# A depthwise-and-pointwise kernel: x's first chunk issued by ScalarE, and 28 satisfied waits on SyncE

## The chip, the cores and the metric

One core of a Trainium2 chip. The metric is the device time of one execution in microseconds (us), as the median of a kernel's runs. The span that the profile shows is about 1.7 us shorter than the device time of the same run (573.7 beside 575.44 us for the kernel before).

## The reference

x is (1, 384, 384, 384), dw is (1, 1, 384), pw is (384, 384), all bf16. With a window of one, the depthwise part is one factor for each channel:

```python
out = x * dw[0, 0]                       # each channel by its factor
return jnp.einsum('bhwc,cd->bhwd', out, pw)
```

The kernel folds dw into pw once, so that the rest is a single matrix product of 147456 rows of x with a 384 x 384 matrix.

## The kernel before

x is cut into 288 supertiles of 512 rows. VectorE transposes each (two halves), TensorE multiplies it with the folded weights (48 matmuls), ScalarE evicts it, SyncE loads and stores. Loads come in groups: the first is cut into chunks of 1, 1, 2, 2 and 4 supertiles so that work can start early, the next 26 are ten supertiles long. Three buffers of ten supertiles hold x, three hold the output.

```python
def load_x(t):
    g, i, off, first, L = chunks[t]
    ...                                   # dst: a slice of X buffer g % 3; src: rows of x
    if i == 0 and g >= NR:                # buffer free again?
        je = g_end[g - NR]
        nc.sync.wait_ge(s_t[je % 2][1], je // 2 + 1)
    nc.sync.dma_start(dst, src).then_inc(s_x[g % NR][i], 16)

def store(t):
    ...
    nc.sync.wait_ge(s_a[je % 2], je // 2 + 2)      # evicted?
    nc.sync.dma_start(dst, src).then_inc(s_o[g % NR], 16)

nc.scalar.dma_start(dw_row[:], ...).then_inc(s_dw, 16)
nc.sync.dma_start(pw_n[:], pw.rearrange("(k p) d -> p k d", p=P)).then_inc(s_pw, 16)
todo = []
for t, (g, i, off, first, L) in enumerate(chunks):
    todo.append((g_end[g - NR] if g >= NR else -1, load_x, t))
    todo.append((first + L + 1, store, t))
for _, f, t in sorted(todo, key=lambda a: a[0]):   # 7 loads first, then stores and loads in turn
    f(t)
...
# TensorE: idle matmuls, dw, idle matmuls, fold, main loop
nc.tensor.wait_ge(s_zero, 1)
idle_work(3)
...                                       # three tiny matmuls turn dw into a column
idle_work(3)
nc.tensor.wait_ge(s_pw, 16)
for k in range(3):                        # the fold: scaled selectors times pw
    nc.tensor.wait_ge(s_sw, k + 1)
    ...                                   # 18 matmuls in all; ScalarE and VectorE evict into w_r
with nc.tensor.Fori(0, NS // 2, 1) as it: # the main loop: 288 supertiles of 48 matmuls
    ...
# ScalarE: two warm copies, five evictions of the fold, then one eviction a supertile
# VectorE: selectors, one eviction of the fold, then two transposes a supertile
```

## Time and profile before

| | us |
|---|---|
| device time, median of 6 runs (lowest, highest) | 575.76 (575.40, 577.48) |
| span of the profiled run | 573.70 |
| pw landed | 4.05 |
| first matmul of the main loop | 7.18 |
| main loop, to the end of its last matmul | 561.81 |
| after it (eviction, last store, barrier) | 4.72 |

The last three rows, the start, the loop and the tail, 7.18 + 561.81 + 4.72, are the span. The prediction below shows the lines of the page, of the chain and of the timeline that carry this. The clock was granted in full in this profile at 6.82 us, before the loop began.

### The profile page before, as it was taken

Reading aid. Unit: us, or ns where it says so; the run is one execution under the profiler, and the core shown is the slowest. Engines: PE = TensorE matmul, PEld = TensorE weight load, DVE = VectorE, ACT = ScalarE, POOL = GpSimd, SP = SyncE. Lnnn points to the kernel's source line nnn. Section 1 sums busy time; section 2 is a strip of 40 time slices with the busy share of each in tenths; the row PEclk is TensorE's granted clock in tenths of the full one; section 3 lists DMA queues with packets and bytes.
Section 4 is the critical chain, followed back from the end, with each engine's and each line's share of the span. In section 5 each row is a group of like instructions: output and inputs, shape, how many; then the busy total and the mean of one; then the engine's idle time right before and its main releaser. Section 6 shows DMA issues by size and latency. Waiting matters only on the chain.

```text
span 573.7 us, 29706 instructions
## 1 busy us (share of the span) xinstructions
PE 567.3 (99%) x13869; PEld 414.9 (72%) x13869; DVE 509.3 (89%) x583; ACT 418.8 (73%) x296; POOL 0.9 (0%) x8
## 2 busy tenths in 40 slices
PE   8999999999999999999999999999999999999996
PEld 5777777777777777777777777777777777777774
DVE  6899999999999999999999999999999999999994
ACT  6777777777777777777777777777777777777775
POOL 0000000000000000000000000000000000000000
PEclk9999999999999999999999999999999999999999
DMA  8999999999999999999999999999999999994996
GB/s 324 432 409 417 430 397 430 444 424 422 399 408 416 384 397 436 398 383 395 432 398 384 395 429 390 393 401 429 402 385 419 401 390 397 425 394 149 402 408 251
DMA packets 25912, 226.88 MB, mean 395 GB/s; under 512 B 1197, under 2 KB 5678, under 8 KB 22062
## 3 DMA queue, kind: packets, MB, share of 16 engines
q1 hardware_dynamic: 25900, 226.79, 98.0%
q14 instruction: 9, 0.07, 0.0%
q8 instruction: 1, 0.02, 0.0%
q10 hardware_dynamic: 2, 0.00, 0.0%
HBM read 113.54 MB, written 113.25 MB: 395 GB/s over the span
## 4 chain that ended last, share of the span: by engine, by line
PE 98%; DMA 1%; ACT 0%; DVE 0%; issue 0%; SPq 0%
PE ps L166 97%; DMA pw_n<-in_pw_dram 1%; PE ps L216 1%; DMA out_dram<-O 0%; ACT O L307 0%; DVE O L304 0%; SPq L337 0%; SPq L100 0%
## 5 line engine op out<-in xcount | busy, mean ns | idle before, releaser
L166 PE MATMUL ps<-w_r,T 32*128 32x384 bf16 x13824 | 561.8, 321 | 0.1
L258 DVE STREAM_TRANSPOSE T<-X 128x384 uint32<-128x384 uint32 x576 | 506.2, 882 | 54.0 <-DMA X<-in_x_dram 2.4
L307 ACT CAST O<-ps 128x1536 bf16<-128x1536 f32 x288 | 413.5, 1436 | 147.9 <-PE ps L166 147.9
L166 PEld LDWEIGHTS ps<-w_r,T 32*128 32x128 bf16 x13824 | 412.9, 93 | 149.2 <-issue 0.7
L271 ACT CAST w_r<-ps 128x768 bf16<-128x768 f32 x5 | 3.7, 805 | 1.7 <-PE ps L216 1.6
L183 PE MATMUL ps<-zero 32*128 32x384 bf16 x24 | 2.6, 494 | 1.4 <-POOL zero L232 1.4
L304 DVE CAST O<-ps 128x768 bf16<-128x768 f32 x1 | 1.0, 958 | 3.0 <-DMA out_dram<-O 3.0
L216 PE MATMUL ps<-pw_n,sel_w 64*128 64x384 bf16 x18 | 3.0, 510 | 0.1
L183 PEld LDWEIGHTS ps<-zero 32*128 32x128 bf16 x24 | 0.7, 100 | 2.6 <-issue 2.6
L216 PEld LDWEIGHTS ps<-pw_n,sel_w 64*128 64x128 bf16 x18 | 1.2, 138 | 1.6 <-issue 1.2
L244 ACT ACT_TABLE_LOAD x1 | 1.3, 1283 | 1.5 <-SPq L100 1.5
L276 DVE TENSOR_REDUCE sel<-eye 128x64 f32<-128x128 bf16 x1 | 0.3, 290 | 1.8 <-POOL eye L234 1.8
L271 DVE CAST w_r<-ps 128x768 bf16<-128x768 f32 x1 | 1.0, 956 | 1.0 <-PE ps L216 1.0
L286 DVE TENSOR_SCALAR sel_w<-sel,dw_f 128x256 bf16<-128x256 f32 x3 | 0.9, 348 | 0.0
L283 DVE COPY dw_f<-ps 128x3 f32<-128x3 f32 x1 | 0.2, 161 | 0.8 <-PE ps L198 0.8
L198 PEld LDWEIGHTS ps<-ones,dw_row 1*128 1x128 bf16 x3 | 0.2, 98 | 0.2 <-issue 0.2
L244 ACT COPY warm<-warm 128x1 f32<-128x1 f32 x2 | 0.3, 188 | 0.0
L234 POOL TENSOR_SCALAR_AFFINE_SELECT eye<-ones 128x128 bf16<-128x128 bf16 x1 | 0.3, 292 | 0.1
L232 POOL MEMSET zero<- 128x192 uint32 x1 | 0.3, 258 | 0.0
L198 PE MATMUL ps<-ones,dw_row 1*128 1x1 bf16 x3 | 0.2, 159 | 0.0
L233 POOL MEMSET ones<- 128x128 bf16 x1 | 0.2, 204 | 0.0
L231 POOL MEMSET warm<- 128x3 f32 x1 | 0.1, 101 | 0.5 <-SPq L100 0.5
(4 smaller groups left out, 0.4 us busy)
## 6 DMA issues: line engine op xcount, KB each, us to landing
X<-in_x_dram SPq DMA_DIRECT2D x26, 3840.0 KB, 21.5
out_dram<-O SPq DMA_DIRECT2D x26, 3840.0 KB, 27.5
X<-in_x_dram SPq DMA_DIRECT2D x2, 1536.0 KB, 17.4
out_dram<-O SPq DMA_DIRECT2D x2, 1536.0 KB, 13.7
X<-in_x_dram SPq DMA_DIRECT2D x3, 768.0 KB, 8.8
out_dram<-O SPq DMA_DIRECT2D x3, 768.0 KB, 8.9
X<-in_x_dram SPq DMA_DIRECT2D x1, 2304.0 KB, 18.9
out_dram<-O SPq DMA_DIRECT2D x1, 2304.0 KB, 12.1
```

The source lines that it names most:

```text
L166: mm = nc.tensor.matmul(PS[s][:, q, :D], lhsT=Ts[s][32 * q : 32 * q + 32, b, par::2], rhs=w_r[32 * q : 32 * q + 32, b, par, :], start=(b, ...
L183: nc.tensor.matmul(PS[0][:, i, :D], lhsT=zero[32 * i : 32 * i + 32, 0:P], rhs=zero[32 * i : 32 * i + 32, :], start=True, stop=True, tile_p ...
L198: mm = nc.tensor.matmul(PS[1][:, 0, D + k : D + k + 1], lhsT=dw_row[:, P * k : P * k + P], rhs=ones[0:1, 0:1], start=True, stop=True,)
L216: mm = nc.tensor.matmul(PS[(k + 1) % 2][:, 2 * r + v, :D], lhsT=sel_w[64 * v : 64 * v + 64, k, r, :, :].rearrange("p q w -> p (q w)"), rhs ...
L232: nc.gpsimd.memset(zero[:].bitcast(U32), 0).then_inc(s_zero)
L234: nc.gpsimd.affine_select(out=eye[:], in_=ones[:], pattern=[[-1, P]], compare_op=mybir.AluOpType.is_equal, fill=0.0, base=0, channel_multi ...
L244: c = nc.scalar.copy(warm[:, s + 1 : s + 2], warm[:, 0:1])
L258: ins = nc.vector.transpose(out=Tw[:, 3 * h : 3 * h + 3], in_=Xw[:, :, j, 96 * h : 96 * h + 96].rearrange("p k (b w) -> p b k w", w=32),)
L271: o = nc.vector.tensor_copy(out, in_) if e == 0 else nc.scalar.copy(out, in_)
L286: nc.vector.tensor_scalar_mul(sel_w[:, k], sel[:].unsqueeze(2).to_broadcast([P, 2, 4, 32]), dw_f[:, k : k + 1]).then_inc(s_sw)
L304: e = nc.vector.tensor_copy(Ov[:, nq:4, j, :], PS[s][:, nq:4, :D])
L307: a = nc.scalar.copy(Ov[:, 0:nq, j, :], PS[s][:, 0:nq, :D])
```

## The change

Its intent is a faster start: ScalarE's queue is free when SyncE has pw and seven loads to issue, so the first chunk of x goes there, and SyncE gets to the second chunk half a microsecond sooner. The 28 waits, all satisfied by then, only lengthen SyncE's program ahead of its first store.

```diff
-        def load_x(t):
+        def load_x(t, eng=nc.sync):
...
-            nc.sync.dma_start(dst, src).then_inc(s_x[g % NR][i], 16)
+            eng.dma_start(dst, src).then_inc(s_x[g % NR][i], 16)
...
         nc.scalar.dma_start(dw_row[:], dw.rearrange("a e c -> a (e c)")).then_inc(s_dw, 16)
+        load_x(0, nc.scalar)
         nc.sync.dma_start(pw_n[:], pw.rearrange("(k p) d -> p k d", p=P)).then_inc(s_pw, 16)
...
-            todo.append((g_end[g - NR] if g >= NR else -1, load_x, t))
+            if t > 0:
+                todo.append((g_end[g - NR] if g >= NR else -1, load_x, t))
...
         for _, f, t in sorted(todo, key=lambda a: a[0]):
+            if f is store and t == 0:
+
+                for _ in range(28):
+                    nc.sync.wait_ge(s_pw, 16)
             f(t)
```

## The prediction

> **What bounds the kernel now.** I read four views of the profile of before, in this order: the page, to see which engine is full; the chain of work that ended last, to see which piece at the start and at the end counts; the busy time in four stretches, to see if the middle has any gap; and the timeline and the waits of the first microseconds, because everything in this change happens there.
>
> The page: TensorE is busy nearly all the time, and the chain that ended last is nearly all one line.
>
> ```profile
> PE 567.3 (99%) x13869; PEld 414.9 (72%) x13869; DVE 509.3 (89%) x583; ACT 418.8 (73%) x296; POOL 0.9 (0%) x8
> ...
> PE ps L166 97%; DMA pw_n<-in_pw_dram 1%; PE ps L216 1%; DMA out_dram<-O 0%; ACT O L307 0%; DVE O L304 0%; SPq L337 0%; SPq L100 0%
> ...
> L166 PE MATMUL ps<-w_r,T 32*128 32x384 bf16 x13824 | 561.8, 321 | 0.1
> L258 DVE STREAM_TRANSPOSE T<-X 128x384 uint32<-128x384 uint32 x576 | 506.2, 882 | 54.0 <-DMA X<-in_x_dram 2.4
> ```
>
> The last column is to be seen: TensorE idles 0.1 us before 13824 matmuls, so no wait inside the main loop costs anything. VectorE idles 54.0 us and is not the bound, although its transposes wait 2.4 us for loads.
>
> The chain in order of time (start, length, piece):
>
> ```profile
> 0.89 0.12 issue
> 1.01 3.03 DMA pw_n<-in_pw_dram
> 4.05 0.05 issue
> 4.09 2.96 PE ps L216 x18
> 7.05 0.12 issue
> 7.18 557.91 PE ps L166 x13728
> 565.08 0.02 issue
> 565.11 1.45 ACT O L307
> 566.55 0.02 issue
> 566.57 2.46 DMA out_dram<-O
> ```
>
> The kernel has three parts. Until 7.18 us it waits for the small matrix pw (issued at 1.01, landed at 4.05) and folds dw into it on TensorE. From 7.18 on it is matmuls alone: 13728 of them are 286 supertiles of 48, and 557.91 / 286 = 1.951 us each. All 288 take 561.8 us and end at 569.0. The rest, 573.7 - 569.0 = 4.7 us, is the last eviction, the last store and the closing barrier. The span is therefore 7.18 + 561.8 + 4.7 = 573.7 us.
>
> The same in stretches (columns: length, then busy time of each engine, then granted clock, DMA share, GB/s):
>
> ```profile
> 4.05:7.18 3.13, 2.96 (x19) 1.25 (x20) 2.23 (x3) 2.45 (x4) 0.00 (x0) 1.00 0.85 264
> 7.18:569.00 561.82, 561.78 (x13824) 412.87 (x13824) 504.80 (x575) 413.96 (x289) 0.00 (x0) 1.00 0.99 400
> ```
>
> TensorE is busy 561.78 of 561.82 us. The middle can get slower, but it can't get faster by moving a load. The DMA engines are full too (0.99), yet their work is ahead of TensorE's by whole buffers.
>
> **What the Trainium skill says.** "DMA: Bandwidth & Descriptors", section "Issuing engines are not separate DMA queues", says that transfers from the scalar and the sync queue run on the same 16 DMA engines and interleave, so that issuing from two engines saves issue time only. The trace before agrees on the size of that saving: consecutive issues on SyncE begin about 0.5 us apart (seven of them in 3.49 us). Section "Queues, rings and completion order" of the same page says that each DMA engine takes turns between the queues that have work, packet by packet. The trace before can't show this, since everything but dw goes through one queue. The prediction's sign rests on it. "TensorE: Matmul & The Clock Gate", section "Part 1: The HAM clock gate", says that TensorE's array runs at half clock until it has been busy for a window of about 3.4 us, and that the window runs free of the kernel's start. The trace agrees: taken one by one, the pairs of folding matmuls at 4.1 to 6.6 us begin 313 ns apart for 384 columns (1.2 columns a ns), and the groups of four in the main loop 162.5 ns apart (2.4 a ns).
>
> **The change, part by part.**
>
> 1. *x's first chunk leaves SyncE's queue.* SyncE's timeline is
>
> ```profile
> 1.01 0.45 SPq L132 DMA_DIRECT2D pw_n<-in_pw_dram  x1
> 1.52 3.49 SPq L113 DMA_DIRECT2D X<-in_x_dram  x7
> 10.82 2.35 SPq L128 DMA_DIRECT2D out_dram<-O  x2
> ```
>
> pw's issue stays at 1.01. The six other loads are issued some 0.5 us earlier. That buys no bytes: behind the issues the DMA engines are already full (0.85 of them busy from 4.05 to 7.18).
>
> 2. *ScalarE issues it after dw.* dw's issue takes 0.97 to 1.46, so x's first chunk is issued at about 1.5, where SyncE issued it at 1.52. ScalarE's own work moves back by one issue, 0.49 us: its table load from 1.49 to about 2.0, its two warm copies to an end at 3.6. Its first needed work, the eviction of the folded weights, starts at 4.63. So 1 us of slack remains and this costs nothing.
>
> 3. *x's first chunk now competes with pw.* This is the part on the path. Taking the DMA packets one by one, pw is 384 packets of 768 B that start from 2.12 on and end by 3.69 us. The chunk is 128 packets of 3072 B at 121 ns, which is 128 x 121 / 16 = 0.97 us of each DMA engine. Before, its first packet starts at 3.01, on an engine that has finished its part of pw. After, if it takes from issue to first packet what pw took (2.12 - 1.01 = 1.1 us), it starts at 1.5 + 1.1 = 2.6 us. By then 91 of pw's 384 packets had started; the other 293 would share with it. At worst all 0.97 us falls ahead of pw's last packets. But between 2.12 and 3.0 us the 229 packets of pw, of 47 ns mean, fill 10.8 of 16 x 0.88 = 14.1 us, so about a quarter of the time is free and takes up part of it. I choose 0.6 us later for pw, out of 0.2 to 1.0. Everything up to the main loop follows pw (0.05 + 2.96 + 0.12 = 3.13 us after it), so the loop starts at about 7.8 and the end moves by the same 0.6 us. Nothing gives it back, since the loop has no gap.
>
> 4. *28 satisfied waits on SyncE.* pw has landed by 4.05 before and by about 4.7 after, and SyncE gets there at about 4.5. Two plain waits at the end of the kernel begin 64 ns apart on SyncE; 28 x 64 = 1.8 us at most, an estimate (fewer if two fold into one instruction). They end near 6.5 us. The first store waits for the first eviction until 10.82, so 4 us of slack is left. Cost: nothing.
>
> Sum: 575.77 + 0.6 = 576.4 us.
>
> **The rivals.**
>
> *Earlier data helps.* The chunk's transposes start at 5.83, but it landed at 5.00: VectorE was busy until then with a folded weight (0.96 us from 4.96). The second chunk is what VectorE waits for:
>
> ```profile
> 8.00 1.57 DVE L258 STREAM_TRANSPOSE T<-X 128x384 uint32<-128x384 uint32 x2 [0.62 <-DMA X<-in_x_dram]
> ```
>
> Its half tile is ready at about 8.8, and the second supertile starts at 7.18 + 1.95 = 9.13, so there's no stall to remove. If pw somehow landed earlier with less queued behind it on its ring, the gain would be 0.1 to 0.3 us: 575.5.
>
> *A load becomes late.* The tightest one is the first long group: it lands at 25.16, its transposed half is ready at about 26.1, and supertile 10 starts at 7.18 + 10 x 1.95 = 26.68. Slack 0.6 us. The bytes ahead of it are the same as before, and a later start of the loop adds slack. I give this little weight; it would cost some tenths of a us.
>
> *The clock gate.* The idle matmuls end at 4.02, just as pw lands at 4.05. If pw is 0.6 us late, TensorE has a hole of that length in the window that should release the clock. If the release then misses its turn, up to 3.4 us of main loop run at half clock, which costs up to 1.7 us: 578.1. The three runs of before spread from 575.57 to 577.48, 1.9 us, which has the size of such a missed window, though no trace here shows that it is one. I give it one chance in six.
>
> *The waits push something else.* They lengthen SyncE's program and can move its instruction fetches. SyncE idles between transfers nearly everywhere, and nothing here reaches 1 us.
>
> **Range and chances.** The low end is no delay of pw plus run-to-run spread (575.3). The high end is 1.0 us of delay with a missed clock window for most of its 1.7 us (578.2). A change of 2% would be 11.5 us; no part of the change touches the 561.8 us of matmuls, so both outer chances are tiny.
>
> **What would show it.** After: the chain's piece for pw is longer than 3.03 us by the same amount by which the main loop starts after 7.18; 48 matmuls still take 1.95 us; the tail after the last matmul is still 4.7 us; SyncE's first store is still issued some 3.6 us after the loop's start. Step 3 is wrong if pw lands by 4.1 us. Step 4 is wrong if the first store comes later than 1.5 us after the first eviction's start. The whole is wrong if TensorE shows waits inside the loop.

## More of the kernel before

All runs that have a state were in the fast one. The five kernels that ran once (e4, e8, e9, e10, e12) have none; I read their profiles, and no verdict rests on their times.

## The result, and the profile after

The kernel after takes 575.87 us (median of 6 runs, 575.26 to 576.42), the kernel before 575.76 us (6 runs). The ratio is 0.9998 with a 95% interval of 0.9985 to 1.0012: no difference is to be seen. A ratio here is the mean time of one kernel's fast runs over the mean of the other's of the same rounds, so it is not quite the ratio of the medians.

The chain of the kernel after, in order of time (start, length, piece), to be held against the chain of before in the prediction:

```profile
...
2.84 1.18 PE ps L189 x12
4.01 3.00 PE ps L222 x18
7.02 0.02 issue
7.04 558.29 PE ps L172 x13728
565.33 0.02 issue
565.35 1.45 ACT O L313
566.80 0.02 issue
566.82 2.45 DMA out_dram<-O
```

The piece "DMA pw_n" is gone from the chain. pw landed at 3.91 us, 0.1 us before the last idle matmuls ended (4.01), so the chain now goes through these; the fold's first weight load still waits for pw and follows its landing by 0.04 us:

```profile
3.95 0.13 PEld L222 LDWEIGHTS ps<-pw_n,sel_w 64*128 64x128 bf16 x4 [0.34 <-DMA pw_n<-in_pw_dram]
```

The loop starts at 7.04, 0.14 us earlier than before, yet the same 13728 matmuls take 558.29 us in place of 557.91.

The stretches of before again, of the kernel after:

```profile
4.05:7.18 3.13, 3.11 (x22) 1.25 (x26) 2.36 (x4) 2.58 (x4) 0.00 (x0) 1.00 1.03 413
7.18:569.00 561.82, 561.82 (x13824) 384.16 (x13816) 503.00 (x575) 414.11 (x289) 0.00 (x0) 1.00 0.99 399
```

TensorE is as full as it was; the loop isn't slower because of a wait. In the first stretch the DMA engines moved 413 GB/s where they had moved 264. So loads did come earlier, which VectorE's timeline shows too:

```profile
4.82 0.96 DVE L277 CAST w_r<-ps 128x768 bf16<-128x768 f32 x1 [0.86 <-PE ps L222]
5.69 6.74 DVE L264 STREAM_TRANSPOSE T<-X 128x384 uint32<-128x384 uint32 x8
```

Eight transposes run without a wait. Before, two ran, then VectorE waited 0.62 us for the second chunk. That chunk landed at 7.97 us before and at 5.86 after; the first one landed later than before (5.58 in place of 5.00). And SyncE:

```profile
1.01 0.45 SPq L133 DMA_DIRECT2D pw_n<-in_pw_dram  x1
1.52 2.89 SPq L113 DMA_DIRECT2D X<-in_x_dram  x6
11.13 2.28 SPq L128 DMA_DIRECT2D out_dram<-O  x2
```

Taken one by one, the waits are 13 instructions of two waits each, 63 ns apart, from 4.47 to 5.25 us; the last two waits went onto the store's own instructions. The first store is issued 0.09 us after the end of the first eviction, where it had been 0.03.

Where the 0.24 us between the two profiles is: the loop's start gave 0.14 us; its first three groups of four matmuls took 272, 320 and 280 ns in place of 162, which cost 0.38 us; the tail is the same (4.71 and 4.72). The clock record explains the slow groups: full clock was granted at 7.87 us, after the loop's start, where before it was 6.82.

### The profile page after: what moved, and what is told of

Read it like the earlier page. It is cut to its first block, busy times and chain, and to the rows that moved or that the text cites. A ratio compares the mean times of both kernels' runs of the same rounds, so it can differ in the third digit from the quotient of the medians.

```text
span 573.9 us, 29720 instructions
## 1 busy us (share of the span) xinstructions
PE 567.8 (99%) x13869; PEld 386.3 (67%) x13869; DVE 507.6 (88%) x583; ACT 419.1 (73%) x296; POOL 0.9 (0%) x8
## 4 chain that ended last, share of the span: by engine, by line
PE 98%; DMA 0%; ACT 0%; DVE 0%; issue 0%; POOL 0%; POOLq 0%; SPq 0%
PE ps L172 97%; PE ps L222 1%; PE ps L189 0%; DMA out_dram<-O 0%; ACT O L313 0%; DVE O L310 0%; POOL zero L238 0%; POOL warm L237 0%; PE ps L204 0%; POOLq L343 0%; SPq L100 0%
## 5 line engine op out<-in xcount | busy, mean ns | idle before, releaser
L172 PEld LDWEIGHTS ps<-w_r,T 32*128 32x128 bf16 x13824 | 384.3, 93 | 178.2 <-issue 0.7
```

Source lines behind the costliest of these rows:

```text
L172: mm = nc.tensor.matmul(PS[s][:, q, :D], lhsT=Ts[s][32 * q : 32 * q + 32, b, par::2], rhs=w_r[32 * q : 32 * q + 32, b, par, :], start=(b, ...
```

## The experiments

Twelve experiments, in three batches and a single one; two are repeats of the two kernels. The record names another chip for each batch (1, 12, 5, and 7 for e12), and each ratio compares runs of one batch. First the table of all profiles, since the argument needs them side by side. "Clock" is when the record shows full clock granted (for e4 and e9, the second time: it had come at 4.90 and 5.83 and was withdrawn in the long wait for data). "Loop" is from its first matmul to the end of its last. All in us; GB/s is what the DMA engines moved from 5 to 8 us.

| kernel | pw landed | clock | loop starts | loop | tail | span | GB/s |
|---|---|---|---|---|---|---|---|
| before | 4.05 | 6.82 | 7.18 | 561.81 | 4.72 | 573.70 | 287 |
| before again (e8) | 4.11 | 7.52 | 7.24 | 561.92 | 7.42 | 576.58 | 338 |
| after | 3.91 | 7.87 | 7.04 | 562.19 | 4.71 | 573.94 | 419 |
| after again (e10) | 3.91 | 4.92 | 7.00 | 561.81 | 4.71 | 573.52 | 428 |
| move only (e1) | 4.04 | 7.62 | 7.17 | 562.00 | 4.82 | 574.00 | 430 |
| waits only (e2) | 3.95 | 4.98 | 6.89 | 561.80 | 5.90 | 574.59 | 270 |
| x before pw (e3) | 5.07 | 7.86 | 8.20 | 561.81 | 5.32 | 575.33 | 287 |
| no idle work (e5) | 3.94 | 9.62 | 7.22 | 562.97 | 4.71 | 574.89 | 281 |
| 400 waits (e6) | 4.10 | 6.32 | 7.23 | 561.81 | 4.72 | 573.76 | 420 |
| pw split (e7) | 4.15, last part | 6.48 | 6.67 | 561.81 | 4.71 | 573.18 | 390 |
| pw split again (e11) | 5.08, last part | 10.89 | 7.38 | 563.51 | 4.71 | 575.60 | 399 |
| long load on ScalarE (e4) | 3.98 | 18.55 | 15.43 | 563.32 | 4.92 | 583.67 | 371 |
| the same, later in program (e9) | 3.94 | 19.49 | 15.63 | 563.68 | 4.83 | 584.14 | 383 |
| small packets first (e12) | 6.82 | 11.27 | 9.95 | 562.43 | 6.14 | 578.53 | 352 |

To be read in it: in every row the span is loop start + loop + tail. The loop is 561.8 us plus, where the clock came after the loop's start, half of the time between, less some 0.04 us: after, (7.87 - 7.04) / 2 = 0.42 against 0.38; no idle work, (9.62 - 7.22) / 2 = 1.20 against 1.16; pw split again, (10.89 - 7.38) / 2 = 1.76 against 1.70.

### e1: the move alone

```diff
-            if f is store and t == 0:
-
-                for _ in range(28):
-                    nc.sync.wait_ge(s_pw, 16)
```

(against the kernel after)

> The move of x's first chunk alone, without the 28 waits. My theory: both parts of the change cost and gain nothing, and the 0.2 us between the two profiles is the phase of TensorE's clock (3 slow groups of four matmuls in the profile after, none before). Then the ratio to before is 1.000 within its interval, pw lands between 3.9 and 4.1 us, x's first packets on ScalarE's queue start only when each DMA engine has ended pw (3.2 us or later), and the loop's length is 561.8 us plus half of whatever part of it ran at half clock. Rival, cancelling parts: the move alone costs or gains some tenths (574.5 or 576.5 us) and the waits give it back. One thing open: the 8 KB instruction fetch seen at 569.07 us before and at 496.8 after is SyncE's if it moves one SyncE instruction later here, to about 570.0, beside the last store; if that stalls the store the tail after the last matmul grows from 4.71 to about 5.0 us.

Measured: 575.49 us (5 runs) beside 575.58 (9 runs of before); ratio 0.9993, interval 0.9979 to 1.0006. pw landed at 4.04, the chunk's first packet on ScalarE's queue started at 3.01, 58 ns after the first of the packets that tell of pw's completion (I had expected 3.2 or later), and two slow groups at the loop's start cost 0.19 us. The instruction fetch was at 570.82, where the profile of before had it at 569.07, and the tail was 4.82, not 5.0. The fetch's place says nothing of the move, since the unchanged kernel has it at 570.83 in e8. The move costs and gains nothing that timing shows.

### e2: the waits alone

```diff
         for _, f, t in sorted(todo, key=lambda a: a[0]):
+            if f is store and t == 0:
+
+                for _ in range(28):
+                    nc.sync.wait_ge(s_pw, 16)
             f(t)
```

(against the kernel before)

> The 28 waits alone, x's first chunk back on SyncE. My theory: ratio to before 1.000 within its interval; 13 or 14 wait instructions some 61 ns apart end near 5.9 us, the first store is issued within 0.15 us of the first eviction's end, and an instruction fetch appears near 480 to 500 us in place of the one at 569 us, with the tail unchanged at 4.7 us. Rival, cancelling parts: this alone is 0.5 us or more away from before, in the opposite direction of the move alone.

Measured: 575.27 us (5 runs) beside 575.58; ratio 0.9990, interval 0.9976 to 1.0003. Again there are 13 wait instructions, ending at 6.04 us, and the first store was issued at 10.60, 0.1 us after the end of the first eviction. SyncE's 8 KB fetch is at 495.88 us, so the waits move it away from the tail, as in the kernel after (496.79). That buys nothing: profiles with the fetch at 569.07, 567.40, 570.20 and 496.79 all have a tail of 4.71 or 4.72 us. This profile's tail was 5.90 because the last store landed late, which other profiles show without the waits (5.32 in e3). Two parts that cancel each other would have opposite signs. The intervals of e1 and e2 end at 0.35 and 0.2 us above before, so such parts could be a few tenths of a microsecond at most, and the profiles show none.

### e3: a control, x's first chunk ahead of pw

```diff
+        load_x(0)
         nc.sync.dma_start(pw_n[:], pw.rearrange("(k p) d -> p k d", p=P)).then_inc(s_pw, 16)
```

(against the kernel before; the chunk is left out of the list)

> A control that delays pw on purpose: x's first chunk is issued before pw on SyncE, so pw is behind its 0.97 us of packets and 0.5 us later in issue. My theory: pw lands at about 5.0 us, the loop starts 3.0 to 3.1 us after that (about 8.1), nothing gives it back, and the time is about 1.0 us above before (576.7), up to 1.7 us more where the clock is released late. Rival, pw is not what the start waits for: the loop starts by 7.4 us and the time stays within 0.3 us of before.

Measured: 576.83 us (5 runs, 576.62 to 577.22) beside 575.58; ratio 1.0017, interval 1.0003 to 1.0031. The chain:

```profile
1.47 3.61 DMA pw_n<-in_pw_dram
5.07 0.05 issue
5.12 2.96 PE ps L218 x18
8.08 0.12 issue
8.20 557.91 PE ps L168 x13728
```

pw is back in the chain. It landed 1.02 us later than in the profile of before, the loop started 1.02 us later, and the medians are 1.25 us apart. So a delay of pw does go through to the end. The timing of the kernel after alone would not have excluded the predicted 0.6 us (its interval goes up to 0.7 us above before); that of e1 does (up to 0.35), and pw's landing shows directly that there was no delay. It is the only timed kernel whose interval excludes 1.

### e4 and e9: a long load on ScalarE's queue

e4 puts the first ten-supertile load (3840 KB) in the place of the first chunk; e9 puts it after ScalarE's warm copies in the program.

```diff
-        load_x(0, nc.scalar)
+        load_x(5, nc.scalar)
...
-            if t > 0:
+            if t != 5:
```

(e4, against e1)

> The load of the first long group (3840 KB, ten supertiles) is issued by ScalarE after dw, the first chunk again by SyncE after pw, no waits: two queues with much work at once. Theory of issue order (whichever queue issued first is served first): the long load is issued at about 1.5 us, a hair before x's first chunk, so that chunk lands after some 9.8 us of the long load's packets, at about 14 us, and the kernel ends some 8 to 9 us later than before (584). Theory of taking turns packet by packet (what I predicted with): x's first chunk lands at about 6 us, the second at about 8, all of SyncE's early loads run at half rate until the long one is done at about 23 us, TensorE stalls only later, before supertile 6, by some 4 to 6 us (580).

Measured: one run, 585.39 us, span 583.67. VectorE and TensorE wait at the start:

```profile
PE ps L168 <- DVE T L260: 9.2, 1, 9.2
DVE T L260 <- DMA X<-in_x_dram: 8.6, 1, 8.6
```

The long load landed at 14.27 us, the first chunk at 14.45. That is the number of the "issue order" theory. Counting packet starts in each microsecond of the trace shows that it is wrong:

```
us         long load (30720 B)   first chunk (3072 B)
4 to 5             15                    14
5 to 6              7                    10
6 to 7             11                     9
7 to 8             15                    13
8 to 9             16                    16
9 to 10            15                    15
```

The two queues take turns, about one packet each. But a packet of the long load takes 1.14 us and one of the chunk 0.12, so the chunk, with as many packets (128), ends only when the long load does. My expectation for "taking turns" had silently assumed packets of equal size.

```diff
             c.then_inc(s_a[s])
+        load_x(5, nc.scalar)
```

(e9, against the kernel before with the load taken out of SyncE's list)

> The 3840 KB load again on ScalarE's queue, but issued after ScalarE's two warm copies, at about 3.1 us, between SyncE's issues of its fourth early load (2.98) and its fifth (3.45). Theory of issue order, now the leading one: the first chunk lands near 5, the second near 7.5, the third near 9.5, the fourth (two supertiles) near 11.5 us, all as before; the long load lands near 21, and only SyncE's fifth load is behind it, near 25 us, so TensorE stalls some 6 us at supertile 6. Rival, ScalarE's queue goes first whenever it has work: the long load lands near 14.5 us and the second, third and fourth chunks all land after 14 us. Rival, taking turns packet by packet: the second to fourth chunks land at about twice their time (10, 14, 18 us) and the long load near 22.

Measured: one run, 585.86 us, span 584.14. The experiment failed as designed: ScalarE's queue issued the load at 1.60 us, not 3.1, since the issue doesn't wait for the table load and the copies ahead of it (they ran until 3.1). So it repeats e4, with the load issued 0.08 us after the chunk and not just before it, and the outcome is the same: landings at 14.46 and 14.65. That the order of two issues so near each other doesn't matter fits taking turns.

### e5: no idle matmuls

```diff
-        nc.tensor.wait_ge(s_zero, 1)
-        idle_work(3)
...
-        idle_work(3)
```

(against the kernel before)

> The kernel before without its two blocks of idle matmuls, to size the clock. So far six profiles show the clock released at 4.9 to 7.9 us, 3.4 to 6.4 us after TensorE's first matmul at 1.43, and what ran after the loop's start at half clock cost half its length. Theory (a free-running window that must be filled by work): with no work before the fold at about 4.05 us, the release falls between 7.4 and 10.9 us; the loop starts at about 7.2 and loses half of what lies between, 0.1 to 1.8 us, 1.0 on average; median about 576.6 us and a wider spread. Rival (the release doesn't follow TensorE's own work): release stays between 4.9 and 7.9 us and the time within 0.2 us of before.

Measured: 576.01 us (6 runs, 575.32 to 576.91) beside 575.52 (11 runs); ratio 0.9998, interval 0.9979 to 1.0018, so timing alone decides nothing. The profile does: clock at 9.62, eight slow groups, the loop 1.16 us longer, inside the 0.1 to 1.8 expected. In this profile the first chunk of x landed late (6.22 us) and set the loop's start; that is a hazard of the original order too.

### e6: 400 waits

```diff
-                for _ in range(28):
+                for _ in range(400):
```

(against the kernel after)

> The changed kernel with 400 satisfied waits in place of 28: 200 wait instructions x 0.061 us = 12.2 us, so SyncE reaches its first store at about 16.7 us in place of 11.1. Theory (the waits are hidden, and even a late first store is): ratio to before 1.000 within its interval, loop still without gaps, tail 4.7 to 5.9 us as in the runs so far. Rival (SyncE's early order matters): the later stores and the fourth long load slip by 5 us, ScalarE or VectorE waits for a buffer, and the time rises by 1 us or more. It is also a third profile with x's first chunk on ScalarE's queue: if the higher DMA rate seen with it between 5 and 8 us (419 and 430 GB/s, against 287, 270 and 287 with all loads on SyncE) belongs to the move, it is above 400 here.

Measured: 575.42 us (4 runs) beside 575.52; ratio 0.9999, interval 0.9972 to 1.0026. The first store was issued at 17.48 us, 6.4 us later than in the kernel after, and the loop is gapless (561.81). The delay is gone by the third long load (the first that reuses a buffer), issued at 32.69 (32.48 before, 32.61 after): the issue of the third store ends only at 30 to 31 us in every case, after 14.6 us before and 11.5 here. What holds it isn't shown. Fourteen times the waits still cost nothing.

### e7 and e11: pw in three parts

```diff
-        nc.sync.dma_start(pw_n[:], pw.rearrange("(k p) d -> p k d", p=P)).then_inc(s_pw, 16)
+        for k, eng in enumerate((nc.sync, nc.scalar, nc.sync)):
+            eng.dma_start(pw_n[:, k, :], pw[P * k : P * k + P, :]).then_inc(s_pw[k], 16)
...
-        idle_work(3)
-        nc.tensor.wait_ge(s_pw, 16)
+        idle_work(1)
...
+            nc.tensor.wait_ge(s_pw[k], 16)
             nc.tensor.wait_ge(s_sw, k + 1)
```

(against the kernel before; s_pw becomes three semaphores)

This is the version that e3 points to: if pw's landing moves the end, an earlier pw should help.

> The kernel before with pw in three transfers of 128 rows, each with its own semaphore, the middle one on ScalarE's queue, and the second idle block cut from 3 rounds to 1. If the start hangs on pw's landing alone, the fold of the first third can begin at about 3.5 us, when its scaled selector is ready (3.43), the loop starts about 0.5 us earlier (6.6 us) and the time falls by 0.5 us to about 575.1, ratio 0.999, which 5 rounds may or may not show. Against it: the third transfer may land later than 4.05 us and the clock's phase moves the loop by up to 0.5 us either way.

> The kernel with pw in three transfers once more, with 5 more rounds. In its first profile the loop started at 6.67 us, 0.51 earlier than before, yet its timed median was 575.94 us. If the gain is there but small beside the spread of tail and clock, the profile again shows a loop start of 6.6 to 6.8 us and the ratio is between 0.998 and 1.000. If the first profile was luck, the loop starts at 7.0 or later.

Measured: e7 575.94 us (6 runs, 574.90 to 576.50), ratio 0.9999, interval 0.9979 to 1.0018; e11 575.69 (6 runs, 574.89 to 577.32) beside 575.55 (11 runs), ratio 0.9998, interval 0.9986 to 1.0011. In e7's profiled run the loop started at 6.67, as expected, and that run took 574.90 us. In e11's it didn't:

```profile
1.52 3.37 DMA pw_n<-in_pw_dram
4.88 0.05 issue
4.93 2.42 PE ps L217 x14
7.35 0.03 issue
7.38 559.61 PE ps L167 x13256
```

One third landed at 4.88 and another at 5.08, the fold's third pair of matmuls began 1.08 us after its second (0.3 us elsewhere), and the clock came only at 10.89 us: 1.70 us of the loop lost, and a run of 577.32. The gain of 0.5 us is there in one profiled run and lost in the other. No version that beats the two kernels came out.

### e8 and e10: the two kernels once more

No edit.

> The kernel before once more, unchanged, for a second profile. Expected: clock released anywhere between 4.8 and 8.2 us, loop 561.8 us plus half of what runs at half clock, tail 4.7 to 5.9 us, and the DMA rate between 5 and 8 us below 300 GB/s if the low rate belongs to the one queue and not to one unlucky run.

Measured: one run of 578.29 us, span 576.58, slower than any of the timed runs of before. Its loop took 561.92 us, so neither clock nor loads made it slow. The wait for the last stores did, which SyncE shows as

```profile
SPq L141 <- DMA out_dram<-O: 4.7, 1, 4.7
```

where the profile of before had 2.0 us. The DMA rate between 5 and 8 us was 338 GB/s, above the 300 that I had set, but well under those of the move.

> The changed kernel once more, unchanged: a fourth profile with x's first chunk on ScalarE's queue. Expected: pw lands at 3.9 to 4.1 us; DMA rate between 5 and 8 us above 400 GB/s; VectorE waits for no load; the time is loop start plus 561.8 us plus half of what runs at half clock plus a tail of 4.7 to 7.4 us, where the tail and the clock vary from run to run as they do with the kernel before.

Measured: one run of 575.24 us, span 573.52. 428 GB/s. Two things differ from what I expected. VectorE did wait for loads, 0.26 us for the first chunk and, in the loop, 0.28 us for the first long load at 23.99 us; TensorE didn't wait for it. And full clock came early, at 4.92, the fold was done by 6.17, and then the first chunk's landing set the loop's start.

```profile
1.52 4.50 DMA X<-in_x_dram
6.02 0.02 issue
6.04 0.87 DVE T L264
6.91 0.09 issue
7.00 557.91 PE ps L172 x13728
```

With the move this chunk shares the engines with the second one and landed at 5.5 to 6.0 us, where with one queue it landed at 4.9 to 5.1 in three profiles (before, e2, e8; 6.2 in e5). In an early-clock run that may cost a tenth: the loop started at 7.00 here and at 6.89 in e2.

### e12: many small packets ahead of pw

```diff
+        nc.sync.dma_start(junk[:, :, 0:96], ...first 384 rows of x in pieces of 192 B...).then_inc(s_junk, 16)
         nc.sync.dma_start(pw_n[:], pw.rearrange("(k p) d -> p k d", p=P)).then_inc(s_pw, 16)
```

(against e1; SyncE waits for s_junk at the end)

> The move alone, with a useless transfer of 1536 packets of 192 B issued on SyncE ahead of pw (nobody waits for it before the end). It asks why x's first chunk never got in among pw's packets, although the run with the long load on ScalarE's queue shows packets of two queues taking strict turns once both are there (16 of one to 16 of the other in a microsecond). In the profiles with the move the chunk's first packet starts 1.5 to 1.8 us after its issue, on each DMA engine only after pw's last. Theory of order in the making of packets (a transfer's packets become ready only after those of every transfer issued earlier, on either queue): the chunk's first packet starts only when the small packets are nearly all through, at 4.5 us or later, and hardly any small packet starts after it on the same engine; pw, issued after both, lands last, at 6 us or later. Rival, a plain delay of 1.5 to 1.8 us from issue to first packet on ScalarE's queue: the chunk's first packet starts at 3.0 to 3.3 us and takes turns with small packets, most of which are still to come then.

Measured: one run, 580.24 us. The first packet of the chunk started at 2.85 us, 1.34 us after its issue, with most of the 1536 small packets still to come. Packet starts in the trace:

```
us            small packets   x's first chunk
2.4 to 2.8        144               0
2.8 to 3.0        159               6
3.0 to 3.3         96              21
3.3 to 3.7         44              48
3.7 to 4.1         54              47
```

So my theory of order in the making of packets fell. A transfer on the other queue does get in among the packets of an earlier one. But not at once: when turns of about one to one set in, at 3.3 us, some 400 small packets had started, about 25 for each of the 16 engines. pw has 384 packets, 24 for each engine. In the profile after, a packet of the chunk starts 5 to 6 ns after each of the sixteen completion packets that end pw, one on an engine. Both fit an engine that works through some two dozen packets that it has already taken in before it turns to the other queue; pw would then be just short enough to slip through. That is a reading of two counts and not a proven mechanism; the first packet of the chunk in e12 got in when 189 small ones, 12 for each engine, had started.

The plain delay on ScalarE's queue, the rival in the expectation, is settled by the traces of e7 and e11. There ScalarE issues a third of pw at 1.52 us, when it issues the chunk in the kernel after. Its first packet started at 2.68 and 2.55 us, when 135 and 125 packets of pw on SyncE's queue had started (the first third has 128, 8 for each engine), and it took turns with SyncE's second third, issued 0.05 us earlier. In the four profiles with the move, with 24 packets of pw ahead on each engine, the first packet came at 3.01 to 3.28. (The third's packets are of 768 B and the chunk's of 3072.) So it was not the queue that was slow but the work ahead of it that came first. A fixed count of two dozen is out too; what fits is all that an engine had been given by then, 8 packets in the one case and 24 in the other.

## Why the prediction was right or wrong

The prediction gave 576.4 us in a range of 575.3 to 578.2, and a change of 2% only a tiny chance. Measured: 575.87. By its own steps:

**Step 1, earlier issues buy no bytes: wrong, without effect.** With the move, four profiles moved 419 to 430 GB/s between 5 and 8 us; with all loads of x on SyncE and pw in one piece, five moved 270 to 338. The lines of before and after for that stretch:

```profile
5.00:8.00 3.00, 2.88 (x35) 1.41 (x35) 2.38 (x4) 2.90 (x5) 0.00 (x0) 1.00 0.83 287
```

```profile
5.00:8.00 3.00, 2.98 (x30) 1.26 (x30) 3.00 (x5) 2.90 (x5) 0.00 (x0) 1.00 1.04 419
```

The load of the first long group landed at 23.8 to 23.9 us with the move and at 24.3 to 25.2 without. In the five slow profiles 12 to 18 packets of 3072 or 6144 B that start between 3 and 9 us take over 0.4 us each (a packet of 3072 B took 0.12 at the median); in the four with the move 0 to 6 do. I took "busy" for "at the full rate": the DMA engines of before were 0.83 busy, in part with slow packets. Why there are such packets stays open, and whether the second queue or the issues half a microsecond earlier removed them was not tested apart. A second queue for pw alone is not enough: from 2 to 8 us e7 and e11 moved 320 and 316 GB/s, the move 357 to 374, and the five others 288 to 327. The gain went where the first rival had said that it would go: off the critical path. VectorE's waits for loads (2.4 us before, 0.8 in its second profile) vanish in the profile after (0.5 in its second, e10), and TensorE never waited for it.

**Step 2, ScalarE has room: right.** Its table load ran from 1.92 and its copies ended at 3.50; the first eviction of the fold was not late.

**Step 3, pw is 0.6 us later: this failed**, by its own sign too (pw by 4.1 us). pw landed at 3.91 us (before: 4.05), and at 3.91 to 4.10 in all four profiles with the move. The step put the chunk's first packet at 2.6 us and let it share with the other 293 packets of pw. In its place the runs showed a first packet at 3.0 to 3.3 us, and on each engine only after pw's last, as far as the times tell (the trace doesn't name the engines). The premise beneath it holds: e4 shows the queues taking turns packet by packet, and e3 shows that a delay of 1.0 us in pw does reach the end. The 1.1 us from issue to first packet holds as well where little is ahead: 1.0 and 1.2 us on ScalarE's queue in e11 and e7. What failed is that a chunk that is ready at 2.6 us shares with the packets of pw that are left: on each engine it came behind all of them, as if they had been taken in before. Why an engine keeps that order is not shown.

**Step 4, the waits are hidden: right.** They take 0.78 us, since two fold into one instruction, and 400 of them cost nothing either. Two of the prediction's signs were missed all the same: the first store came 1.53 us after the first eviction's start, where 1.5 was the limit (1.46 before), and 4.1 us after the loop's start in place of 3.6, of which the slow groups are 0.4. The limit was too tight; e6 settles the step.

**The rival of the clock gate: right in kind, wrong in what it explained.** The loop does lose half of what it runs before full clock, 0.38 us in the profile after and 1.70 us in e11. But e3 had a hole of 1.1 us before the fold and lost nothing, so a hole in TensorE's work alone doesn't settle it: in the profiles with the idle work and pw in one piece (e12 aside, where pw was 2.8 us late) the first release came anywhere from 4.9 to 7.9 us. The clock records tell more. In every profile the changes of the clock lie whole multiples of 3.413 us apart (before: 6.82 and 573.43 us, 166 of them; e4: 4.90, 8.31 and 18.55), and where these steps lie differs from profile to profile. In 13 of the 14 profiles the first release came at the end of the first step of 3.413 us in which TensorE was busy for 3.09 us or more, and steps with up to 3.03 us of work passed without one (in e11 one with 2.86 us, after a hole of 0.5 us in the fold). e3, released after a step with 2.74 us, doesn't fit, so busy time is not the whole rule. And I likened the spread of the runs of before (1.9 us) to one missed window. The one slow run of before that was profiled (e8) owes 2.7 us to the last store's landing and 0.1 us to the clock.

One small reading was off: the pairs of folding matmuls begin 320 ns apart and not 313 (the first two 291). So the range held the result by its low end, which had allowed for no delay of pw, and not by step 3: the 0.6 us that set the middle of it were not there. The 0.1 us between the two medians is inside the noise, and nothing should be read into it.

## What to carry to other kernels

When TensorE has no gap from the first matmul of the loop to the last, write the time as start + loop + tail and ask of each part of a change which of the three it moves; here the move made the second chunk land 2.1 us earlier, yet the loop started at 7.00 to 7.23 us in the four profiles with the move and at 7.18 and 7.24 in the two of before, and it had no gap in either. In e4 a transfer on a second queue took turns with the first by packets and not by bytes, so a transfer with small packets that the start depends on should not run beside one with large packets. Before explaining half a microsecond, profile the same kernel twice: here the clock took up to 1.7 us of the loop and the last store 2.7 us of the tail.

## What the Trainium skill lacked or had wrong

- "DMA: Bandwidth & Descriptors", "Queues, rings and completion order": it says that engines take turns between queues by packet. The runs agree (44 to 48 and 54 to 47 packets in 0.4 us in e12), but it doesn't say that the turns ignore size (a packet of 30720 B took 1.14 us, one of 3072 B 0.12, about one to one in e4), or when a second queue gets its first turn: behind 24 packets of the first for each engine in the kernel after, behind 8 in e7 and e11. Its packet holds several descriptors; whether the trace counts in the same unit is not shown.
- The same page, "Rules for kernel authors": spreading transfers over engines is said not to help bandwidth. From 5 to 8 us of this kernel the profiles with the move had more, 419 to 430 GB/s against 270 to 338; that the second queue is the reason was not tested apart. From 8 to 12 us both ways gave 433 to 444.
- "TensorE: Matmul & The Clock Gate", "Part 1: The HAM clock gate": the release is put at about 4 us of sustained work, 0.5 us either way. With matmuls from 1.43 us on and holes of 1.1 us at most, it came 3.5 to 6.4 us after the first one, and in e11 9.5 us. The spread is nearly a whole step of 3.413 us, the smallest distance of the clock's changes in these traces, and not of half a microsecond either way.
- No page that I read gives the spread of the last store's landing: SyncE's wait for it was 2.0 to 2.2 us in ten profiles, 2.6 to 3.3 in three and 4.7 in one (e8), where it is the largest part of the lost time.
